# Query-key normed attention on one core: sums of squares on TensorE, four norm steps on GpSimd, a 22-column v, and another plan

## Chip, cores and metric

The kernel runs on one core of a Trainium2 chip. The metric is the device time of one execution in microseconds (us); where several runs were made, their median.

## What is computed

The reference normalizes q and k by their lengths over the last axis, multiplies the logits by a temperature per head, and does plain attention. There are 32 heads, 2048 rows and 20 columns per head; all inputs are bf16.

```python
qn = q / (jnp.sqrt((q * q).sum(axis=-1, keepdims=True)) + eps)
kn = k / (jnp.sqrt((k * k).sum(axis=-1, keepdims=True)) + eps)
logits = jnp.einsum('bhqd,bhkd->bhqk', qn, kn) * t[None, :, None, None]
attn = _softmax(logits, axis=-1)
return jnp.einsum('bhqk,bhkd->bhqd', attn, v)
```

## The kernel before

**Tiles.** Four heads form a group, so there are 8 groups; a group has 4 blocks of 512 queries. One unit of work is one head, one block of 512 queries and one strip of 128 keys: 8 x 4 x 4 x 16 = 2048 units. For each unit TensorE multiplies 128 keys by 512 queries (L692) into a bank of 512 fp32 columns. The columns of a head are padded from 20 to 32, so that four heads lie side by side on the 128 rows of `qT` and `kT`.

**Two ways to the exponential.** A unit takes one of two ways. In the first ("A"), two units form a wave in `psA`, and ScalarE turns the wave's 1024 columns into `pA` in one call (L885). In the second ("D"), the unit goes to one of three banks of `psD`; VectorE forms an int16 whose bits, read as fp16, are a rough exponential (`P1`, L325, result in `dI`), and two copies of it with a constant added (`S1` and `S2`, results in `dS`) mend the shape. These additions, called shifts below, are done by VectorE (L340, several units in one call) or by GpSimd (L338, as int32, so 256 columns for a unit's 512). The product with v (L714, "PV") is one matmul for an A unit and four for a D unit: `dI` with v, `dI` with half of v (`vhalf`), and the two `dS` with v. All of them add up in `psO`, 32 rows per head: 20 columns of v, one column of ones for the denominator, and zeros. At the end of a block VectorE transposes `psO` out (`drain`, L360), takes a reciprocal (`rec`, L364), and GpSimd multiplies (`omul`, L366).

**The preparation of a group** (`prep_ops`) is done while the group before it is computed: squares (`sq`, L260) and their sums over 20 columns (`red`, L263) on VectorE, eight small steps on 128 sums (`rs0` to `rs5`, `eps`, `inv`, L282 to L289) on VectorE, the scaling of k and q (L304) on GpSimd, and two DMA transposes issued from SP (L414). For the first group a shorter path through ScalarE's square root gets the first 512 rows going.

**A plan fixes the order.** `make_plan` runs through the kernel once in Python, with a clock of its own and a price for each operation, and from this it writes out one fixed order of instructions for each engine, with semaphore waits where data demand it. `step_pe0` picks the next matmuls, `step_dve` and `step_pool` the next work of VectorE and GpSimd, `step_sp` the next DMA. Two rules matter here. VectorE calls that read SBUF at more than one column per cycle keep GpSimd off SBUF (`o.port`); so the plan starts a GpSimd operation only beside a VectorE call that reads PSUM (`P1`, `drain`) and adds a wait for the call before that one. And small filler matmuls (`heat`, L558) are put in where TensorE would have too little to do, to keep its clock up. Which units go the D way is not written down anywhere: it comes out of the plan.

**Constants.** `NPA` is the number of `pA` slots, `RUN_MAX` the most units in one VectorE shift, `POOL_MAX` the most in one GpSimd shift, `PSLACK` how far a GpSimd operation may stand out beyond the VectorE call beside it, `PREP0`, `PREPN`, `PREP1` when the preparation is spread in, `LOAD1` when the loads of the second group start.

Of the kernel before, what the change touches and what calls it, by code (L numbers as in the profile page):

```python
# [6 lines left out]
BF16 = mybir.dt.bfloat16  # L7
# [34 lines left out]
PREP1 = (.25,.35)  # L42
# [3 lines left out]
HOLD = 0  # L46
# [7 lines left out]
POOL_MAX = 3  # L54
ALONE = (.2, 0)
PMIN = 5
PGAP = 0.3
PVHOLD = (.22,.22)
HEAT0 = 11
HEATN = 128  # L60
HEAT = .57
# [4 lines left out]
ACT0 = .05  # L66
ACT1 = .24
# [10 lines left out]
PSLACK = 0.15  # L78
# [3 lines left out]
SOON = 8  # L82
DURG = 1
LOAD1 = 0.2
DJOIN = 0.3
# [60 lines left out]
def bass_standalone__qk_norm__prompt_kernel(  # L146
# [15 lines left out]
    with ExitStack() as es:  # L162
# [16 lines left out]
        vaug = [sbuf(f"vaug{i}", [128, NH, R, 32], BF16) for i in range(2)]  # L179
        vpart = {c: [sbuf(f"v{n}{i}", [128, NH, R, 32], BF16) for i in range(2)] for c, n in ((.5, "half"),)}  # L180
# [7 lines left out]
        idn = sbuf("idn", [128, 128], BF16)  # L188
        nr0 = sbuf("nr0", [128, 2, NH, 4], F32)
# [41 lines left out]
        def prep_ops(hg, r0, r1, a0=0, a1=2, pool=False):  # L231
# [9 lines left out]
            for c0 in range(r0, r1, sqn * 2 // na):  # L241
# [30 lines left out]
            def add(nm, emit, reads, writes, rate=R1, fix=0.0):  # L272
                ops.append(dve(nm, n, rate, emit, reads, writes, fix))
# [5 lines left out]
            else:  # L279

                y = ri.bitcast(F32)
                add("rs0", lambda e: e.tensor_scalar(ri, s_.bitcast(I32), -0.5, RS_MAGIC, ALU.mult, ALU.add), [SS], [K("ri")], R2)  # L282
                add("rs1", lambda e: e.tensor_tensor(rb, s_, y, ALU.mult), [K("ri"), SS], [K("rb")])
# [58 lines left out]
        def part_op(hg, c):  # L342
            b = hg % 2
            f = lambda tl: tl[b][:, :, :, :].rearrange("p h r d -> p (h r d)")
            return dve("vh", NH * R * 32, R4, lambda e: e.tensor_single_scalar(f(vpart[c]), f(vaug), c, ALU.mult),
                       [("v", b, hh) for hh in range(NH)] + [("vz", b)], [("vh", b, c)])
# [33 lines left out]
        def load_qk(hg, a, part=None):  # L380
            b = hg % 2
            r0, r1 = (0, R) if part is None else PARTS[part]
            if a == 0 and hg == HG - 1:

                ops = []
                for x in range(4):
# [10 lines left out]
                        0.5, 4.0 if part != 0 else 2.2)]  # L397
# [10 lines left out]
        def tr_op(hg, which, r0, r1):  # L408
# [6 lines left out]
                       [(which + "pad", b, r) for r in range(r0, r1)], keys, 0.58 + 0.17 * (r1 - r0), 1.75 + 0.17 * (r1 - r0))  # L415
# [21 lines left out]
        def make_plan(share):  # L437
# [61 lines left out]
            def zeros(i, after=()):  # L499
                z = lambda ap_, val, key: Op("POOL", "z", lambda e: e.memset(ap_, val), after, [(key, i)], 0.5, 0.6)  # L500
                return [z(kpad[i][:, :, :, D:32], 0.0, "kz"), z(qpad[i][:, :, :, D:32], 0.0, "qz"),
                        z(vaug[i][:, :, :, D:D + 1], 1.0, "vz"), z(vaug[i][:, :, :, D + 1:32], 0.0, "vz")]
# [3 lines left out]
                               [], ["iot"], 0.5, 0.6)] + zeros(0))  # L506
# [54 lines left out]
            o = Op("PE", "heat", None, ["zt"], [("psA", 0)])  # L561
            o.info = [(lambda e, i=i: e.matmul(psA[:, (i % 3) * QW:(i % 3 + 1) * QW], zt[:, 0:128], zt[:, :])) for i in range(HEAT0)]
# [56 lines left out]
            if share:  # L619
                for c in vpart:  # L620
                    o = part_op(0, c)
                    o.reads.append(("qpad", 0, R - 1))
                    want_dve(o, 3)
            loaded = 1
            next_prep = []
            first_prep = [x[2] for x in dve_todo if x[2].name not in ("cp", "vh", "z")]
# [4 lines left out]
            def plan_group(hg):  # L631
# [9 lines left out]
                w_ = [o.cost if o.eng == "DVE" else PREPW * o.cost for o in po]  # L641
# [4 lines left out]
            def feed_prep():  # L646
                while next_prep:
# [10 lines left out]
                    want_dve(o, PRIO)  # L658
                    next_prep.pop(0)

# [6 lines left out]
            def pe_put(op, mode, strips):  # L667
# [5 lines left out]
                for hh in strips:  # L673
                    s0 = max(st, grp[hh])
                    grp[hh] = s0 + TS
# [5 lines left out]
                used_w.append((st, end, 0.25 * TS * len(strips) / (end - st)))  # L681
# [27 lines left out]
            def pv_mm(unit, rhs, first, last, coef):  # L709
# [3 lines left out]
                dst = psO[32 * hh:32 * hh + 32, :]  # L713
# [122 lines left out]
            def step_pe0():  # L836
# [73 lines left out]
                if pe_mode != "qk" and flying < DURG and not 0 < wait < DJOIN and step_qkd([], False):  # L910
                    return True
                if parts and not slot_free and before is not None and before.done is not None \
# [16 lines left out]

            def psd_free_at():  # L930
                rds = P.readers.get(("psD", issued_d % DBANKS), [])
# [4 lines left out]
            def step_qkd(used, with_a):  # L936
# [13 lines left out]
                def empty(i):  # L950
                    rds = P.readers.get(("psD", i), [])
                    return all(r.done is not None and r.done + SEML <= now for r in rds) and (rds or P.last_w.get(("psD", i)) is None)
# [379 lines left out]
```

## Time and profile before

| what | value |
|---|---|
| time, median of 3 runs | 632.86 us (632.52 to 632.88) |
| the profiled execution | 633.45 us |
| its span, first to last instruction | 631.5 us |
| granted TensorE clock, mean | 0.995 of full speed |
| units by ScalarE / by VectorE | 1333 / 715 |
| shifts (units x 2): VectorE / GpSimd | 703 / 727 |
| filler matmuls of 128 columns | 310 |

The page lists each engine's busy time, then groups of equal instructions by source line with their count, busy time, mean duration, and the idle time of the engine just before them with what ended it. "Busy" is the union of the intervals of a group, so it is smaller than count times mean where one call begins before the last has drained. The views by form keep tiles of different sizes apart. The profile's source lines are those of the kernel before; in the changed kernel ScalarE's exponential is L959, `P1` L356, the shifts L371 and L369, QK L766, PV L788 and the filler L591.

### The profile page before, as it was taken

What the parts mean: (1) busy time and instruction counts of PE and PEld (TensorE: products, weight loads), DVE (VectorE), ACT (ScalarE), POOL (GpSimd) and SP (SyncE); (2) the same over time, 40 slices, a digit from 0 to 9 for tenths busy, and PEclk for the clock granted to TensorE, in tenths of its full rate; (3) what the DMA queues carried; (4) which work ended last, traced back from release to release, by engine and by line L of the source; (5) the groups of instructions that cost most, each with busy time, mean ns of one, the idle gap of its engine ahead of it and who ended that gap; (6) DMA issues with size and microseconds to landing.
All of it is one profiled execution on the core that took longest, in us unless ns stands there. A gap on an engine that the chain in (4) does not pass through costs nothing.

```text
span 631.5 us, 15864 instructions
## 1 busy us (share of the span) xinstructions
PE 614.5 (97%) x6794; PEld 180.3 (29%) x6794; DVE 614.1 (97%) x869; ACT 618.8 (98%) x675; POOL 445.5 (71%) x491
## 2 busy tenths in 40 slices
PE   8999999999999999999999999999999999999996
PEld 4432222322222232223223222232222332222221
DVE  6999999999999999999999999999999999999995
ACT  6999999999999999999999999999999999999995
POOL 4586667766677776876768666776777777666772
PEclk8999999999999999999999999999999999999999
DMA  6610404041040130306031050400404022010000
GB/s 73 88 10 16 95 1 43 2 62 48 2 43 2 35 76 5 39 2 111 1 29 16 1 110 3 40 4 3 93 3 57 2 33 37 1 23 6 6 5 13
DMA packets 113772, 19.57 MB, mean 31 GB/s; under 512 B 102944, under 2 KB 113696, under 8 KB 113696
## 3 DMA queue, kind: packets, MB, share of 16 engines
q1 hardware_dynamic: 112896, 18.37, 19.9%
q8 instruction: 55, 0.90, 0.6%
q10 hardware_dynamic: 800, 0.12, 0.1%
q14 instruction: 21, 0.17, 0.1%
HBM read 7.87 MB, written 2.62 MB: 17 GB/s over the span
## 4 chain that ended last, share of the span: by engine, by line
ACT 72%; PE 26%; DVE 1%; DMA 0%; issue 0%; POOL 0%
ACT pA L885 72%; PE psO L714 12%; PE psA L692 10%; PE psD L692 2%; PE psO L558 2%; DMA qk<-in_q_dram 0%; DVE ssum L263 0%; POOL kpad L304 0%; DVE accT L360 0%; PE psD L570 0%; DVE sqs L260 0%; DVE ost L368 0%; DVE qT L585 0%; DVE rn L289 0%; DVE rec L364 0%
## 5 line engine op out<-in xcount | busy, mean ns | idle before, releaser
L885 ACT ACTIVATE pA<-psA 128x1024 f16<-128x1024 f32 (+1 forms) x667 | 614.5, 1111 | 2.0 <-PE psA L692 1.6
L338 POOL TENSOR_TENSOR dS<-dI,shc 128x256 int32<-128x256 int32 (+2 forms) x378 | 373.0, 1007 | 130.0 <-DVE dS L340 93.2
L325 DVE TENSOR_SCALAR dI<-psD 128x1024 int16<-128x1024 f32 (+1 forms) x486 | 434.1, 927 | 4.4 <-PE psD L692 1.8
L692 PE MATMUL psA<-qT,kT 32*128 32x512 bf16 x1553 | 283.0, 384 | 8.9 <-ACT pA L885 6.0
L714 PE MATMUL psO<-pA,vaug 128*32 128x512 f16 (+1 forms) x1333 | 233.7, 384 | 0.0
L714 PE MATMUL psO<-dS,vaug 128*32 128x512 f16 x1430 | 224.5, 385 | 0.0
L692 PE MATMUL psD<-qT,kT 32*128 32x512 bf16 x715 | 193.9, 383 | 0.0
L714 PE MATMUL psO<-dI,vaug 128*32 128x512 f16 x715 | 155.3, 386 | 0.0
L714 PE MATMUL psO<-dI,vhalf 128*32 128x512 f16 x715 | 152.0, 384 | 0.0
L692 PEld LDWEIGHTS psA<-qT,kT 32*128 32x128 bf16 x1553 | 69.0, 91 | 239.4 <-ACT pA L885 224.1
L340 DVE TENSOR_SCALAR dS<-dI 128x2048 int16<-128x2048 int16 (+2 forms) x182 | 122.5, 679 | 0.0
L714 PEld LDWEIGHTS psO<-dS,vaug 128*32 128x32 bf16 x1430 | 51.1, 94 | 73.2 <-issue 58.7
L714 PEld LDWEIGHTS psO<-pA,vaug 128*32 128x32 bf16 x1333 | 52.5, 94 | 37.5 <-issue 31.8
L692 PEld LDWEIGHTS psD<-qT,kT 32*128 32x128 bf16 x715 | 45.4, 91 | 22.1 <-DVE dI L325 10.2
L714 PEld LDWEIGHTS psO<-dI,vaug 128*32 128x32 bf16 x715 | 36.7, 93 | 24.5 <-issue 17.4
L714 PEld LDWEIGHTS psO<-dI,vhalf 128*32 128x32 bf16 x715 | 36.4, 94 | 22.0 <-issue 19.2
L366 POOL TENSOR_TENSOR ost<-accT,rec 128x320 bf16<-128x320 f32 x31 | 23.3, 753 | 16.7 <-DVE dS L340 9.5
L304 POOL TENSOR_TENSOR qpad<-qk,rn 128x320 bf16<-128x320 bf16 x31 | 22.0, 728 | 17.3 <-DVE dS L340 10.4
L558 PE MATMUL psO<-zt 128*128 128x128 bf16 x310 | 32.3, 228 | 0.1
L304 POOL TENSOR_TENSOR kpad<-qk,rn 128x320 bf16<-128x320 bf16 x31 | 22.2, 738 | 10.8 <-DVE dS L340 6.1
L558 PEld LDWEIGHTS psO<-zt 128*128 128x128 bf16 x310 | 19.7, 101 | 21.0 <-issue 20.1
L360 DVE STREAM_TRANSPOSE accT<-psO 128x512 f32<-128x512 f32 x32 | 22.6, 705 | 2.7 <-PE psO L714 2.7
(51 smaller groups left out, 100.1 us busy)
## 6 DMA issues: line engine op xcount, KB each, us to landing
vaug<-in_v_dram SPq DMA_DIRECT2D x32, 80.0 KB, 4.0
qk<-in_k_dram SPq DMA_DIRECT2D x7, 320.0 KB, 4.0
out_dram<-ost SPq DMA_DIRECT2D x28, 80.0 KB, 1.9
qk<-in_q_dram SPq DMA_DIRECT2D x6, 320.0 KB, 3.9
qk<-in_q_dram SPq DMA_DIRECT2D x4, 80.0 KB, 3.1
out_dram<-ost SPq DMA_DIRECT2D x7, 40.0 KB, 2.0
qk<-in_k_dram SPq DMA_DIRECT2D x1, 240.0 KB, 3.6
qk<-in_q_dram SPq DMA_DIRECT2D x1, 240.0 KB, 4.2
```

The costliest lines, as they stand in the source:

```text
L304: emit = lambda e, o=dst, x=src, s=sc: e.tensor_tensor(o, x, s, ALU.mult)
L325: lambda e: e.tensor_scalar(dst, psD[:, pb * QW:(pb + n) * QW], 1024.0 * LOG2E, 15360.0 - 1024.0 * LOG2K + SHIFTS[0], ALU.mult, ALU.add),
L338: lambda e: e.tensor_tensor(o.bitcast(I32), x.bitcast(I32), c, ALU.add), rd + ["shc"], wr)
L340: lambda e: e.tensor_single_scalar(o, x, float(SHIFTS[i] - SHIFTS[0]), ALU.add), rd, wr)
L360: dve("drain", QW, R1, lambda e: e.transpose(aT[:, :, :].rearrange("p b d -> p (b d)"), psO[:, :]), ["psO"], [("accT", b)], 0.03),
L366: pool_op("omul", 320, True, lambda e: e.tensor_tensor(dst, num, rcb, ALU.mult), [("accT", b), ("rec", b)], [("ost", ob, qg)]) if pool else
L558: return lambda e: e.matmul(bank, zt[:, 0:128], zt[:, 0:n], start=False, stop=False, skip_group_check=True)
L692: return lambda e: e.matmul(dst, lhsT, rhs, tile_position=(32 * hh, 0))
L714: return lambda e: e.matmul(dst, lhsT, rhs, start=first, stop=last, skip_group_check=True, tile_position=(0, 32 * hh))
L885: a = Op("ACT", "exp", lambda e, s=src, d=dst: e.activation(d, s, ACT.Exp), [("psA", slot)], [("pA", pslot, i) for i in range(WAVES[slot]) ...
```

## The change

- **Sums of squares on TensorE** for groups 1 to 7. VectorE still squares (two calls of 1280 columns per group), the squares go through two DMA transposes (`Ts`, SP queue) into `sqT`, and 20 matmuls of 32 columns against a 0/1 matrix `ind` add them up into a bank of `psD`, which is lent for that and given back when `rs0` and `rs1` have read it. The two `red` calls per group are gone. `ind` is made once at the start from an iota on GpSimd and two small VectorE calls.
- **Four norm steps on GpSimd** (`rs2`, `rs3`, `rs4`, `eps`) for these seven groups.
- **v in 22 columns** instead of 32: 20, the ones, and one zero. The rows 22 to 31 of each head in `psO` are never written by PV; a filler matmul at the very start writes zeros there.
- **The plan** gets GpSimd's late start (`PLAG`, and the end of the VectorE call before), an earlier release of VectorE (`LOCKL`), other prices for DMA (`LOAD0`, `TRL`, `TRK`), and other constants.
- **What comes out of the plan** (instructions on the path that runs):

| engine | instruction | before | after |
|---|---|---|---|
| ScalarE | exponential, 1024 / 512 columns | 666 / 1 | 662 / 0 |
| VectorE | `P1`, 1024 / 512 columns | 229 / 257 | 183 / 358 |
| VectorE | shifts: calls / units | 182 / 703 | 208 / 797 |
| GpSimd | shifts: calls / units | 378 / 727 | 454 / 651 |
| GpSimd | norm steps of 128 columns | 0 | 28 |
| TensorE | PV | 4193 | 4220 |
| TensorE | QK into psA / psD | 1553 / 715 | 1560 / 724 |
| TensorE | filler, 128 columns | 310 + 11 long | 188 + 12 long |
| TensorE | sums, 32 columns | 0 | 140 |
| SP | DMA transposes | 16 | 30 |

At the start, VectorE's order becomes squares, maximum over t (`flag`), sums, two calls for `ind`, `eps`; it was squares, sums, `flag`, `eps`. On SP the four loads of v for the second group now stand ahead of the first DMA transpose of `kT`, and the loads of its k and q ahead of those. On GpSimd a load of the operation library stands ahead of the first `rs3`; the kernel before has one such load, ahead of its iota.

```diff
-NPA = 20
+NPA = 18
+VW = 22
-RUN_MAX = 4
+RUN_MAX = 6
-D_END = 6
-D_LAST = 18
-D_WAIT = 36
+D_END = 4
+D_LAST = 14
+D_WAIT = 30
-PREP1 = (.25,.35)
+PREP1 = (.15,.45)
-POOL_MAX = 3
-ALONE = (.2, 0)
+POOL_MAX = 2
+ALONE = (.2,.2)
+LOAD0 = 2.75
+TRL = 2.25
+TRK = 1.2
+PLAG = .03
+LOCKL = 0.12
-PSLACK = 0.15
+PSLACK = 0.3
-LOAD1 = 0.2
+LOAD1 = 0
+NORM_POOL = ('rs2', 'rs3', 'rs4', 'eps')
...
-            for c0 in range(r0, r1, sqn * 2 // na):
+            bank = {}
+            for a in (1, 0) if hg else ():
+
+                sq, x3 = sqs[a][:, :], qk[b][:, a, :, :, :].rearrange("p h r d -> p (h r d)")
+                w_ = NH * R * D
+                keys = [("sqs", a)] + [("sqs", a, c) for c in range(R)]
+                ops.append(dve("sq", w_, R2, lambda e, o=sq, x=x3: e.tensor_tensor(o, x, x, ALU.mult),
+                               [("qk", b, a, i) for i in parts] + [("qkx", b, i) for i in range(1, 4)] * (a == 0), keys))
+                n_ = w_ // 128
+                dst = sqT[:, a * w_:(a + 1) * w_].rearrange("p (r n) -> p r n", n=128)
+                ops.append(dma("Ts", lambda e, o=dst, x=sq: e.dma_start_transpose(o, x), keys[:1], [("sqT", a)],
+                               0.58 + 0.17 * n_, TRL + 0.17 * n_))
...
             def add(nm, emit, reads, writes, rate=R1, fix=0.0):
-                ops.append(dve(nm, n, rate, emit, reads, writes, fix))
+                ops.append(pool_op(nm, n, rate != R2, emit, reads, writes) if pool and nm in NORM_POOL else
+                           dve(nm, n, rate, emit, reads, writes, fix))
...
+            def step_sums():
+                o = sums_todo[0]
+                for a in range(2):
+                    t_ = P.last_w[("sqT", a)]
+                    if t_.done is None or t_.done + SEML > now:
+                        return False
+                if "at" not in o:
+                    pb = next_bank()
+                    if not empty(pb):
+                        return False
+                    o["at"] = pb
+                    lent[0] += 1
+                    on_loan[:] = [o]
+                g, js = o["left"].pop(0)
+                dst = psD[:, o["at"] * QW + 32 * g:o["at"] * QW + 32 * g + 32]
+                mms = [lambda e, j=j: e.matmul(dst, sqT[:, (5 * g + j) * 128:(5 * g + j + 1) * 128], ind[:, 32 * j:32 * j + 32],
+                                               start=j == 0, stop=j == 4, skip_group_check=True) for j in js]
...
-                dst = psO[32 * hh:32 * hh + 32, :]
+                dst = psO[32 * hh:32 * hh + VW, :]
...
-                fits = lambda c: not busy or now + c <= end + PSLACK
+                st = max(now, on[-2].done + SEML + PLAG) if busy and len(on) > 1 else now
+                fits = lambda c: not busy or st + c <= end + PSLACK
...
-                finish(o, now, o.cost, o.lat)
-                free_["POOL"] = lock[0] = now + o.cost
+                finish(o, st, o.cost, o.lat)
+                free_["POOL"], lock[0] = st + o.cost, st + o.cost - LOCKL
```

More of the change, by code (lines that the diff above doesn't have):

```diff
@@ L45 @@
 DFIRST = 1
-HOLD = 0
+HOLD = 0.2
 DT = 0.005
@@ L640, in plan_group @@
                     po += [part_op(hg, c) for c in vpart]
-                w_ = [o.cost if o.eng == "DVE" else PREPW * o.cost for o in po]
+                w_ = [0 if isinstance(o, dict) else o.cost if o.eng == "DVE" else PREPW * o.cost if o.eng == "POOL" else 0 for o in po]
                 for j, o in enumerate(po):
@@ L949, in step_qkd @@
                     return False
[L950 to L953 removed]
+                pb = next_bank()
                 if not empty(pb):
```

96 lines of the change are left out of this document (72 added, 24 removed).

## The prediction

> **What bounds the kernel now.** I read the page's busy times first, then the groups of calls, then the waits.
>
> ```profile
> span 631.5 us, 15864 instructions
> PE 614.5 (97%) x6794; PEld 180.3 (29%) x6794; DVE 614.1 (97%) x869; ACT 618.8 (98%) x675; POOL 445.5 (71%) x491
> L885 ACT ACTIVATE pA<-psA 128x1024 f16<-128x1024 f32 (+1 forms) x667 | 614.5, 1111 | 2.0 <-PE psA L692 1.6
> ```
> ```profile
> L885 ACT ACTIVATE pA<-psA 128x512 f16<-128x512 f32 x1 | 0.7, 739 | 0.0
> ```
> ```profile
> 20.00:600.00 580.00, 571.89 (x6348) 164.77 (x6351) 576.08 (x788) 579.38 (x629) 421.00 (x453) 1.00 0.20 31
> ```
> ```profile
> PEld psA L692 <- ACT pA L885: 224.1, 552, 0.8
> ```
>
> Three engines show 97% or more, so shares don't name the bound. ScalarE's exponentials do: 667 calls, 614.5 us busy, and only 2.0 us of idle time before all of them. They run back to back, one per 614.5 / 666.5 = 0.922 us (counting the half-wide one as half). A kernel with the same calls can't end much sooner; one with fewer calls can. TensorE isn't the bound although it shows 97%: its weight loads waited 224.1 us for ScalarE to free `psA`, 0.34 us per wave. VectorE is nearly one: between 20 and 600 us (in the window's row its busy time is the third, ScalarE's the fourth) it idled 580 - 576.08 = 3.9 us, ScalarE 0.6 us. So the two are balanced to under 1%, and the plan's split of units is what balances them.
>
> **Term 1, the exponentials: -4.2 us.** The new plan sends 724 units to VectorE, so ScalarE makes 662 wide calls instead of 666 wide and one half-wide. A wide one is worth 0.922 us; the half-wide saves its shorter duration, 1.111 - 0.739 = 0.37, so it is worth 0.55. 4 x 0.922 + 0.55 = 4.24 us. It counts in full only as long as ScalarE stays fed.
>
> **Term 2, the start: +0.5 us.** The chain to the first exponential goes over VectorE.
>
> ```profile
> 1.28 0.48 SPq L529 DMA_DIRECT2D tb<-in_t_dram  x1
> 3.44 0.49 DVE L260 TENSOR_TENSOR sqs<-qk 128x640 bf16<-128x640 bf16 x1 [1.06 <-DMA qk<-in_q_dram]
> 3.97 0.82 DVE L263 TENSOR_REDUCE ssum<-sqs 128x32 f32<-128x640 bf16 x1
> 4.70 0.18 DVE L530 TENSOR_REDUCE tmx<-tb 128x1 f32<-128x32 bf16 x1
> 5.08 0.18 DVE L278 TENSOR_SCALAR rsa<-nr 128x32 f32<-128x32 f32 x1 [0.20 <-ACT nr L277]
> 8.39 1.94 ACT L885 ACTIVATE pA<-psA 128x1024 bf16<-128x1024 f32 x2 [0.32 <-PE psA L692]
> ```
> ```profile
> tb<-in_t_dram SPq DMA_DIRECT2D x1, 8.0 KB, 2.9
> ```
>
> Before, the sums began at 3.97, right behind the squares. Now `flag` stands between, and it waits for the load of t: issued at 1.28, landed 2.9 later, at 4.18. With its own 0.18 the sums begin near 4.40, 0.43 late. Behind them the two calls for `ind` (160 columns, about 0.3 and 0.25 us, an estimate from the 128-column rows of L286 and L285 below) end near 5.65, while `eps` would be ready at 4.40 + (5.08 - 3.97) = 5.51. So `eps` starts at about 5.6 instead of 5.08, and everything behind it moves: the scaling, the transposes, the first exponential. I take +0.5; bounds 0 (t lands before the squares end) and +0.75 (no call overlaps the next).
>
> **Term 3, VectorE's ledger: +0.4 us.** Its changed calls, by these rows:
>
> ```profile
> L325 DVE TENSOR_SCALAR dI<-psD 128x1024 int16<-128x1024 f32 x229 | 277.2, 1211 | 2.6 <-PE psD L692 1.3 <-PE psA L692 0.5
> L325 DVE TENSOR_SCALAR dI<-psD 128x512 int16<-128x512 f32 x257 | 171.7, 674 | 1.8 <-PE psO L558 0.8 <-PE psD L692 0.5
> L340 DVE TENSOR_SCALAR dS<-dI 128x2048 int16<-128x2048 int16 x165 | 114.3, 697 | 0.0
> L340 DVE TENSOR_SCALAR dS<-dI 128x1024 int16<-128x1024 int16 x8 | 3.4, 428 | 0.0
> L263 DVE TENSOR_REDUCE ssum<-sqs 128x64 f32<-128x1280 bf16 x14 | 20.6, 1474 | 0.0
> L286 DVE TENSOR_TENSOR ssum<-ssum,rsa 128x128 f32<-128x128 f32 x7 | 2.0, 291 | 0.0
> L284 DVE TENSOR_TENSOR rsa<-rsb,rsi 128x128 f32<-128x128 f32 x7 | 2.0, 285 | 0.0
> L285 DVE TENSOR_SCALAR ssum<-rsa 128x128 f32<-128x128 f32 x7 | 1.6, 227 | 0.0
> L288 DVE TENSOR_SCALAR rsa<-rsb 128x128 f32<-128x128 f32 x7 | 1.5, 221 | 0.0
> ```
> ```profile
> 149.36 0.68 DVE L340 TENSOR_SCALAR dS<-dI 128x2048 int16<-128x2048 int16 x1
> 149.96 1.81 DVE L325 TENSOR_SCALAR dI<-psD 128x1024 int16<-128x1024 f32 x2
> 151.69 0.68 DVE L340 TENSOR_SCALAR dS<-dI 128x2048 int16<-128x2048 int16 x1
> ```
>
> The timeline shows that a call starts 0.07 to 0.08 us before the last one has ended: a 2048 shift lasts 0.68 and holds the engine 0.60; a 1024 and a 512 `P1` together hold it 1.73, about 1.13 and 0.60. So I count each mean less 0.07:
> - `P1`: 101 more of 512 columns x 0.60, 46 fewer of 1024 x 1.13: +8.6.
> - Shifts: a unit costs (0.697 - 0.428) / 2 = 0.134 us. 94 more units x 0.134 and 26 more calls x 0.07: +14.4.
> - `red`: 14 x 1.40 gone: -19.6.
> - Four norm steps gone: 7 x (0.291 + 0.285 + 0.227 + 0.221 - 0.28) = -5.2.
> - `vhalf` on 640 fewer columns: 8 x 640 / 512 x 0.134 = -1.3.
> - `rs0` now from PSUM, no row for it: taken as 0.1 more than now, +0.7 (bounds 0 and 7 x 0.2); `ind` +0.5.
>
> The sum is -1.9 us, while ScalarE's work shrinks by 4.2. To keep up, VectorE must give up 4.2 - 1.9 = 2.3 us of the 3.9 us that it idled. If it gives all, the term is 0; if none, +2.3. I take +0.4, near the lower end: the idle time was waits for TensorE's `psD`, and TensorE has slack per wave.
>
> **What else moves.** *TensorE* gains 140 small matmuls, 27 PV and some switches and loses 122 fillers.
>
> ```profile
> L570 PE MATMUL psD<-idn,kpad 128*128 128x128 bf16 x4 | 0.4, 222 | 1.1 <-POOL kpad L304 1.1
> 19.55 0.45 PE L558 MATMUL psO<-zt 128*128 128x128 bf16 x5
> ```
>
> Four transposes behind one another took (0.4 - 0.222) / 3 = 0.06 us each, five fillers (0.45 - 0.23) / 4 = 0.055. So 140 x 0.06 - 122 x 0.055 + 27 / 4 x 0.38 (four heads at once, each as long as the QK in the row below, an upper bound) = +4 us, and some 28 changes of mode. The 224.1 us in which the weight loads waited cover it; uncovered, 4 us over 662 waves is 0.006 each. The 22-column weights change nothing that streams: PV still moves 512 columns.
>
> *DMA.* Fourteen transposes join SP's queue; TensorE's sums wait for them, and behind the sums stand QK and PV.
>
> ```profile
> 2.83 6.07 SPq L405 DMA_DIRECT2D vaug<-in_v_dram  x4
> 23.69 0.90 SPq L395 DMA_DIRECT2D qk<-in_k_dram  x1
> 25.20 6.68 SPq L405 DMA_DIRECT2D vaug<-in_v_dram  x4
> 21.38 0.38 PE L692 MATMUL psD<-qT,kT 32*128 32x512 bf16 x1
> ```
> ```profile
> DMA to landing us min/median/max: 3.7/4.3/6.0
> ```
>
> A transpose landed in 3.7 to 6.0 us (8 to 16 blocks); the plan reckons 2.25 + 10 x 0.17 = 3.95 for one of 10. A late one may stop TensorE by up to 2 us, of which the two waves in `psA` cover 1.84: 7 x 0 to 0.2, I take +0.1. The first `kT` transpose is now queued behind the second group's loads: v of the first ends at 8.90, k and q take 1.51 (23.69 to 25.20), four v 6.1 to 6.7, so it is issued near 16.8 and lands at 21.1 to 22.8. TensorE first needs it at 21.38 + 0.5 (the QK in the row, with the start's delay). Bounds 0 and +0.9; covered by the waves in `psA`, I take 0.
>
> *GpSimd* isn't the bound, but the shifts come from it.
>
> ```profile
> L338 POOL TENSOR_TENSOR dS<-dI,shc 128x768 int32<-128x768 int32 x113 | 165.2, 1466 | 70.8 <-DVE dS L340 45.6 <-DVE sqs L260 9.7 <-DVE rsb L283 2.5
> L338 POOL TENSOR_TENSOR dS<-dI,shc 128x512 int32<-128x512 int32 x123 | 127.7, 1039 | 47.9 <-DVE dS L340 39.5 <-DVE vhalf L345 2.4 <-DVE sqs L260 1.8
> L338 POOL TENSOR_TENSOR dS<-dI,shc 128x256 int32<-128x256 int32 x142 | 85.7, 612 | 11.3 <-DVE dS L340 8.1 <-DVE ssum L286 1.2 <-DVE ssum L285 1.0
> L315 POOL TENSOR_TENSOR rn<-rn,tb 128x64 f32<-128x64 f32 x7 | 2.3, 330 | 0.0
> ```
>
> Shifts: 257 x 0.612 + 197 x 1.039 = 362 us against 379 (165.2 + 127.7 + 85.7). The 28 norm steps of 128 columns lie between 0.330 (64 columns) and 0.612 (256): at 0.42 they cost 12. Net -5 us; their latency lies in a preparation that has most of a group's 75 us. I take 0.
>
> One more instruction stands in its queue: a load of the operation library, ahead of the first `rs3`.
>
> ```profile
> 0.83 0.24 POOL L504 IOTA iot<- 128x128 f32 x1 [0.39 <-POOLq L1317]
> ```
>
> The load that the kernel has now, ahead of the iota, left 0.39 us of idle time, and the iota took 0.24. I take 0 (bounds 0 and 0.39; GpSimd idles 130 us beside its shifts).
>
> **The sum**, against the profiled execution: 633.45 - 4.24 + 0.5 + 0.4 + 0.1 = 630.2 us. The median of the runs stood 0.6 below it, so I forecast **629.6 us**.
>
> **Rivals.**
> *A, VectorE is the bound.* It gives up none of its idle time: -1.9 + 0.5 = -1.4, so 632.0 profiled, **631.4** as median. For it: 99.3% busy between 20 and 600 us. Against: its idle time is made of waits, and ScalarE's 0.922 paces those too.
> *B, GpSimd is held by the library load.* The second load comes in mid run, and TensorE stops at a PV whose `dS` is late. By the nearest row (0.39 us) nothing is seen: **629.6**. In a sentence by itself: the Trainium skill, "GPSIMD Engine Reference", section "2.1 Instruction dispatch", says that the first call after a freshly loaded library pays about 6 us with no visible instruction; by that, an estimate, 5.95 - 1.84 of cover = +4.1 and 633.7 us. The trace so far speaks against it, since the iota followed its load within 0.39 us, though the library may have been there already.
> *C, slower: VectorE's shifts wait for GpSimd.* More and smaller GpSimd operations may stand out beyond the `P1` beside them, and the shift that follows on VectorE, which shares SBUF's port with GpSimd, is held. There are 208 such shifts.
>
> ```profile
> 299.53 1.81 DVE L325 TENSOR_SCALAR dI<-psD 128x1024 int16<-128x1024 f32 x2
> 299.69 1.47 POOL L338 TENSOR_TENSOR dS<-dI,shc 128x768 int32<-128x768 int32 x1 [0.72 <-DVE dS L340]
> ```
>
> An undisturbed 2048 shift takes 0.68, the mean is 0.697: 0.017 us is lost per shift now. At 0.03 more per shift it is 208 x 0.03 = 6.2, so -1.4 + 6.2 = +4.8: **637.7**. It makes the kernel slower from (1.4 + 1.3) / 208 = 0.013 us per shift on. Against it: GpSimd starts 0.16 us after the `P1` (row above); the old plan ignored that and let it stand out 0.15, the new one reckons 0.156 and allows 0.30, so the real overhang is the same.
>
> **From this to the numbers.** Within 0.2% (1.27 us) a measurement of this kernel can't tell a change. Forecast 0.50, A 0.20, B as the page has it 0.07, C 0.18, and 0.05 for better than the forecast (ScalarE's idle time at the start gone too, 628). Faster than 631.6: the forecast, the better case and most of A, 0.69; slower than 634.1: C and a little of B, 0.20; between them 0.11. The range 627.8 to 634.0 takes in the bounds of the terms, A, and B; the forecast's own is 628.6 to 630.8.
>
> **What would show it.** Right: 662 exponentials with 2 to 3.5 us of idle time before them, 0.92 us each; the first starting near 8.9 instead of 8.39; `P1` rows with no more idle time than now; no idle stretch on GpSimd at `rs3`. Wrong: over 5 us of idle time before the exponentials; 2048 shifts with a mean well over 0.70; weight loads for `ind` waiting on a DMA for microseconds; a PV waiting on `dS` near 45 us.

## The result and the profile after

| | before | after |
|---|---|---|
| median of 20 runs each, us | 632.79 | 637.07 |
| spread, us | 631.97 to 633.89 | 631.64 and up; one run took 2704.77 |
| ratio after / before, 95% interval | | 1.0057 [1.0040, 1.0074] |
| profiled execution, us (span) | 633.45 (631.5) | 644.17 (642.3) |

The changed kernel is slower by 0.6%, where 629.6 us was forecast. No trace shows what the run of 2704.77 us did; the median is not moved by it. The ratio is taken over the 16 faster executions of after, whose granted TensorE clock was 0.978 to 0.992; the profiled one, with 0.967, is among the slower, 7.1 us above the median, and so shows more of what follows than most runs have.

The granted clock in 40 slices, in tenths of full speed, on the page of before:

```profile
PEclk8999999999999999999999999999999999999999
```

The page of after: the span, the busy times, the granted clock, and the groups of the exponentials and of VectorE's `P1` (busy time, mean ns, then the idle time before them and who ended it).

```profile
span 642.3 us, 16161 instructions
PE 621.7 (97%) x6856; PEld 171.7 (27%) x6856; DVE 614.5 (96%) x910; ACT 617.6 (96%) x670; POOL 442.7 (69%) x596
PEclk9979999999996999999999799999999979999998
L959 ACT ACTIVATE pA<-psA 128x1024 f16<-128x1024 f32 (+1 forms) x662 | 613.3, 1100 | 13.0 <-PE psD L766 8.4
L356 DVE TENSOR_SCALAR dI<-psD 128x512 int16<-128x512 f32 (+1 forms) x541 | 440.6, 853 | 15.2 <-PE psD L766 13.1
```

The exponentials are 662, as planned, but they stood idle for 13.0 us, against 2.0 before, and both they and `P1` waited for TensorE. The clock row says why: four dips inside the span, where before has none behind its first slice. The windows of after show one of them (start and end, length, busy time of PE, PEld, DVE, ACT and POOL with counts, then the granted clock, the DMA share and GB/s):

```profile
186.00:188.00 2.00, 1.80 (x21) 0.72 (x19) 2.00 (x4) 2.00 (x3) 1.65 (x2) 1.00 0.00 0
188.00:190.00 2.00, 1.77 (x28) 0.92 (x26) 2.00 (x4) 2.00 (x3) 1.04 (x1) 1.00 0.00 0
190.00:192.00 2.00, 1.77 (x21) 0.54 (x18) 2.00 (x6) 2.00 (x3) 1.04 (x1) 0.72 0.03 8
192.00:194.00 2.00, 2.00 (x12) 0.41 (x9) 1.40 (x3) 1.73 (x3) 1.45 (x2) 0.50 0.02 4
```

TensorE's timeline in after at the same place (start, duration, operation, count; in brackets a wait and who ended it):

```profile
188.00 0.39 PE L788 MATMUL psO<-pA,vaug 128*22 128x512 f16 x2
188.32 0.29 PE L725 MATMUL psD<-ind,sqT 128*128 128x32 bf16 x5
188.55 0.39 PE L766 MATMUL psA<-qT,kT 32*128 32x512 bf16 x2
188.87 0.29 PE L725 MATMUL psD<-ind,sqT 128*128 128x32 bf16 x5
189.01 0.22 PE L591 MATMUL psO<-zt 128*128 128x128 bf16 x1
189.45 0.39 PE L766 MATMUL psA<-qT,kT 32*128 32x512 bf16 x2 [0.23 <-ACT pA L959]
189.53 0.39 PE L766 MATMUL psD<-qT,kT 32*128 32x512 bf16 x2
189.85 0.29 PE L725 MATMUL psD<-ind,sqT 128*128 128x32 bf16 x5
190.36 0.39 PE L766 MATMUL psA<-qT,kT 32*128 32x512 bf16 x2 [0.23 <-ACT pA L959]
190.69 0.29 PE L725 MATMUL psD<-ind,sqT 128*128 128x32 bf16 x5
190.91 0.60 PE L788 MATMUL psO<-dS,vaug 128*22 128x512 f16 x1
```

This is where the four groups of sums of squares run, one group per wave of exponentials. From the first group to the last a wave holds a pair of QK into `psA`, five matmuls of 32 columns, and in all one filler and one pair of QK into `psD`; there is no PV between 188.4 and 190.9. No wait longer than 0.23 us stands in these lines. Right behind the fourth group a matmul of 512 columns takes 0.60 us instead of 0.39: the clock has fallen to half. It stays there until about 204.5. TensorE is then busy all the time, and ScalarE waits for it, as its timeline in after shows at the first of the four places:

```profile
43.54 1.02 ACT L959 ACTIVATE pA<-psA 128x1024 f16<-128x1024 f32 x1 [0.51 <-PE psA L766]
45.05 1.02 ACT L959 ACTIVATE pA<-psA 128x1024 f16<-128x1024 f32 x1 [0.48 <-PE psD L766]
```

A wave that took 0.92 us takes 1.5. The four falls (40 to 48, 190 to 206, 350 to 362 and 522 to 530 us) each begin at one of the seven stretches of sums and hold 11.6 of the 13.0 us that ScalarE idled. Between them nothing is wrong (windows of after, same columns):

```profile
50.00:186.00 136.00, 133.81 (x1541) 36.12 (x1537) 135.74 (x194) 135.81 (x148) 96.54 (x128) 1.00 0.30 46
530.00:632.00 102.00, 100.56 (x1175) 26.79 (x1169) 101.56 (x141) 102.00 (x112) 76.52 (x102) 1.00 0.09 18
```

ScalarE works 135.81 of 136.00 and 102.00 of 102.00 us.

One more wait of after lies outside of the falls, near 22 us. Rows of its timeline, on SyncE's queue, TensorE and ScalarE:

```profile
18.05 2.16 SPq L445 DMA_TRANSPOSE kT<-kpad  x1
22.20 0.37 PE L766 MATMUL psD<-qT,kT 32*128 32x512 bf16 x1 [1.15 <-DVE dI L356]
22.65 3.77 ACT L959 ACTIVATE pA<-psA 128x1024 f16<-128x1024 f32 x4 [0.55 <-PE psD L766]
```

The first `kT` transpose is issued at 18.05. TensorE's QK on the second group's keys starts only at 22.20, after 1.15 us of idling; the bracket names `P1`, but the wait was for the transpose: it landed 4.0 us after its issue, at 22.05, while the bank was free near 20.9 (the same QK starts at 20.98 in h1_start, further on, where the transpose is issued at 13.92). ScalarE lost 0.55 us.

### The profile page after: what moved, and what is told of

Read it like the earlier page. It is cut to its first block, busy times and chain, and to the rows that moved or that the text cites. A ratio compares the mean times of both kernels' runs of the same rounds, so it can differ in the third digit from the quotient of the medians.

```text
span 642.3 us, 16161 instructions
## 1 busy us (share of the span) xinstructions
PE 621.7 (97%) x6856; PEld 171.7 (27%) x6856; DVE 614.5 (96%) x910; ACT 617.6 (96%) x670; POOL 442.7 (69%) x596
## 3 DMA queue, kind: packets, MB, share of 16 engines
HBM read 7.87 MB, written 2.62 MB: 16 GB/s over the span
## 4 chain that ended last, share of the span: by engine, by line
ACT 64%; PE 27%; DVE 6%; SPq 1%; DMA 1%; issue 0%
ACT pA L959 64%; PE psO L788 13%; PE psA L766 12%; DVE dI L356 4%; DVE dS L371 1%; PE psD L766 1%; PE psO L591 1%; SPq L436 1%; DMA vaug<-in_v_dram 1%; DVE accT L391 0%; SPq L426 0%; PE psD L725 0%; DVE vhalf L376 0%; DVE ost L399 0%; SPq L562 0%
## 5 line engine op out<-in xcount | busy, mean ns | idle before, releaser
L356 DVE TENSOR_SCALAR dI<-psD 128x512 int16<-128x512 f32 (+1 forms) x541 | 440.6, 853 | 15.2 <-PE psD L766 13.1
L369 POOL TENSOR_TENSOR dS<-dI,shc 128x512 int32<-128x512 int32 (+1 forms) x454 | 358.2, 797 | 136.0 <-DVE dS L371 93.2
L766 PE MATMUL psA<-qT,kT 32*128 32x512 bf16 x1560 | 288.5, 392 | 10.2 <-ACT pA L959 7.1
L788 PE MATMUL psO<-pA,vaug 128*22 128x512 f16 (+1 forms) x1324 | 249.9, 389 | 0.5 <-DMA vaug<-in_v_dram 0.5
L788 PE MATMUL psO<-dS,vaug 128*22 128x512 f16 x1448 | 240.0, 390 | 0.1
L788 PE MATMUL psO<-dI,vaug 128*22 128x512 f16 x724 | 167.9, 392 | 0.3
L788 PE MATMUL psO<-dI,vhalf 128*22 128x512 f16 x724 | 167.6, 391 | 0.0
L371 DVE TENSOR_SCALAR dS<-dI 128x3072 int16<-128x3072 int16 (+5 forms) x208 | 140.2, 687 | 0.1
L766 PEld LDWEIGHTS psA<-qT,kT 32*128 32x128 bf16 x1560 | 69.9, 92 | 259.2 <-ACT pA L959 232.4
L788 PEld LDWEIGHTS psO<-dS,vaug 128*22 128x22 bf16 x1448 | 50.6, 89 | 77.1 <-issue 64.9
L788 PEld LDWEIGHTS psO<-pA,vaug 128*22 128x22 bf16 x1324 | 50.9, 89 | 36.0 <-issue 29.7
L788 PEld LDWEIGHTS psO<-dI,vaug 128*22 128x22 bf16 x724 | 36.7, 89 | 27.0 <-issue 15.2
L788 PEld LDWEIGHTS psO<-dI,vhalf 128*22 128x22 bf16 x724 | 37.3, 90 | 22.8 <-issue 20.2
L335 POOL TENSOR_TENSOR qpad<-qk,rn 128x320 bf16<-128x320 bf16 x31 | 22.1, 727 | 16.8 <-DVE dS L371 10.9
```

Source lines behind the costliest of these rows:

```text
L335: emit = lambda e, o=dst, x=src, s=sc: e.tensor_tensor(o, x, s, ALU.mult)
L356: lambda e: e.tensor_scalar(dst, psD[:, pb * QW:(pb + n) * QW], 1024.0 * LOG2E, 15360.0 - 1024.0 * LOG2K + SHIFTS[0], ALU.mult, ALU.add),
L369: lambda e: e.tensor_tensor(o.bitcast(I32), x.bitcast(I32), c, ALU.add), rd + ["shc"], wr)
L371: lambda e: e.tensor_single_scalar(o, x, float(SHIFTS[i] - SHIFTS[0]), ALU.add), rd, wr)
L766: return lambda e: e.matmul(dst, lhsT, rhs, tile_position=(32 * hh, 0))
L788: return lambda e: e.matmul(dst, lhsT, rhs, start=first, stop=last, skip_group_check=True, tile_position=(0, 32 * hh))
```

## The experiments

Theory S: the stretches of sums are too thin to hold TensorE's clock, and all that the change lost is there. Its rivals: the 22-column weights of PV let the clock go (C); something else of the change, VectorE or GpSimd, costs the time, and the falls come by chance. Each ratio is against the kernel before, run in the same session.

**The changed kernel again (e0_after).** No edit.

> The changed kernel as it is. In the profiled execution TensorE's granted clock fell to half four times, for 5 to 15 us each, and each fall began while the four groups of sums matmuls ran. Theory S (the sums stretch leaves TensorE with too little work, and the clock gate halves its clock): falls again, in some of the seven sums stretches and nowhere else, mean clock below 0.992, time 633 to 640 us and different from run to run. Theory C (PV with 22 instead of 32 weight columns counts as less activity): falls too, but not bound to the sums. Rival C of the prediction (VectorE's shifts are held by GpSimd): a mean of the 2048 shifts and of P1 above those of before also where the clock is full.

Measured: 637.4 us median, ratio 1.0071 [1.0041, 1.0102]. In the profiled execution the clock fell at 42 to 48 and 346 to 362 us, both at sums, and once more near the start, at 9 to 13 us, where the profile of before has a fall too (8 to 11 us). So behind the start the falls return at the same kind of place, but not at each place each time. The "nowhere else" of the expectation does not hold for the start.

**Fillers beside the sums (e1_fill).** Same plan and order as after. Behind each of the 28 groups of sums stand two matmuls on zeros, 256 columns each, into an unused part of the bank that the sums have on loan:

```diff
-                op.info = mms
+                rest = psD[:, o["at"] * QW + 256:o["at"] * QW + 512]
+                op.info = mms + 2 * [lambda e: e.matmul(rest, zt[:, 0:128], zt[:, 0:256], start=True, stop=True, skip_group_check=True)]
```

> Same plan and same order on every engine; behind each of the 28 groups of sums matmuls stand two filler matmuls of 256 columns, which write zeros into unused columns of the lent bank (0.21 us of TensorE time each pair). S: no falls of the clock (0.995 as before the change), 629.5 us (629.0 to 630.3), faster than the kernel before by 0.4 to 0.6%. C: the falls stay, or most of them, 633 us or more. Rival C of the prediction: as slow as the changed kernel.

Measured: 630.58 us, 0.3 above the expected range, ratio 0.9962 [0.9942, 0.9983]. More work on TensorE made the kernel 6.8 us faster than e0_after, and faster than before. The page of e1_fill:

```profile
span 628.6 us, 16273 instructions
PE 611.1 (97%) x6912; PEld 172.4 (27%) x6912; DVE 613.9 (98%) x910; ACT 615.8 (98%) x670; POOL 442.3 (70%) x596
PEclk9999999999999999999999999999999999999999
L960 ACT ACTIVATE pA<-psA 128x1024 f16<-128x1024 f32 (+1 forms) x662 | 611.5, 1099 | 1.9 <-PE psA L767 1.3
L356 DVE TENSOR_SCALAR dI<-psD 128x512 int16<-128x512 f32 (+1 forms) x541 | 439.6, 854 | 2.5 <-PE psD L767 0.9
```

No dip in the clock row, 1.9 us of idle time before the same 662 exponentials instead of 13.0, and `P1` waits 2.5 instead of 15.2. Theory S is shown: fillers at the sums and nowhere else, and the loss is gone. The clock isn't safe in every run: ten of the 12 had 0.995 or more, the other two 0.992 and 0.988 (632.82 and 635.47 us), as one of the 29 runs of before had 0.987 (638.34 us). Where these three fell, no trace shows.

**A quarter of the dose (f4_small_fill).** One filler of 128 columns per group:

```diff
-                op.info = mms + 2 * [lambda e: e.matmul(rest, zt[:, 0:128], zt[:, 0:256], ...)]
+                op.info = mms + 1 * [lambda e: e.matmul(rest, zt[:, 0:128], zt[:, 0:128], ...)]
```

> The plan of e1_fill and after, with one filler of 128 columns per group of sums (28 in all) instead of two of 256, a quarter of the columns. If what counts is TensorE's busy share over a stretch, a filler of 0.055 us in waves of 0.92 us moves it by 6 points against 23 in e1_fill (two of about 0.11): the clock still falls to 0.5 in some of the four places, median 634 to 637, ratio 1.002 to 1.006. If any streamed matmul of 128 rows and 128 columns in the wave keeps the clock: 630.6, ratio 0.996, no fall.

Measured: 630.75 us, ratio 0.9978 [0.9964, 0.9992], and no fall in the profiled execution before its end. The median is that of the second expectation. But 5 of its 12 runs had a granted clock under 0.994 (631.2 to 633.9 us), against 2 of 12 with the larger fillers and all 7 of e0_after. It is far from e0_after; 5 against 2 is too few to tell it from e1_fill. The thinnest 2 us in the same stretch, windows of f4_small_fill, of e1_fill and of after:

```profile
187.00:189.00 2.00, 1.74 (x29) 0.86 (x25) 2.00 (x5) 2.00 (x4) 1.10 (x2) 1.00 0.00 0
```
```profile
187.00:189.00 2.00, 2.00 (x30) 1.01 (x28) 2.00 (x5) 2.00 (x4) 1.10 (x2) 1.00 0.00 0
```
```profile
189.00:191.00 2.00, 1.55 (x26) 0.82 (x24) 2.00 (x5) 2.00 (x4) 1.10 (x2) 0.96 0.03 8
```

PE is busy 1.74, 2.00 and 1.55 of 2.00 us. This share doesn't decide a single stretch, though: in after the clock held behind the stretch at 124 us, whose last 2 us had 1.52, and in i3_heat70, further on, it fell where PE was busy 1.90. What amount of work is enough isn't shown.

**v in 32 columns again (e2_v32).** The planner still reckons with 22, so that the order stays the same.

```diff
-VW = 22
+VW = 32
...
-            return dve("vh", NH * R * VW, R4, ...
+            return dve("vh", NH * R * 22, R4, ...
```

> Same plan and order, but v and half v have 32 columns again (zeros in the last 11), so PV loads 32 weight columns. S: no help, 634 to 639 us with falls in the sums stretches. C: no falls, 629.5 to 630.5 us.

Measured: 638.66 us, ratio 1.0099 [1.0061, 1.0137], with falls at 40 to 48 and 190 to 206 us, both at sums. The 22 columns aren't the cause: C is out.

**Sums back on VectorE (e3_dve_sums).** The rest of the change is kept; planned anew it has 718 units and 665 exponentials.

```diff
-            for a in (1, 0) if hg else ():
+            for a in ():
...
-            if hg:
-                ops.append(bank)
-            for c0 in range(r0, r1, sqn * 2 // na) if not hg else ():
+            for c0 in range(r0, r1, sqn * 2 // na):
...
-                sums = lambda: psD[:, ...].rearrange("p (h r) -> p h r", r=R) if hg else s_
+                sums = lambda: psD[:, ...].rearrange("p (h r) -> p h r", r=R) if "at" in bank else s_
```

> The sums of squares go back to VectorE for all groups (no transposes of squares, no sums matmuls, no lent bank); all else of the change stays. The plan then has 718 units for VectorE and 665 exponentials. S: no falls of the clock, 629.5 + 3 x 0.92 = 632.3 us (631.5 to 633). C: falls stay, 635 us or more. Rival C of the prediction: slower than 634 with a full clock.

Measured: 637.2 us, ratio 1.0069 [1.0041, 1.0096]; the expectation is missed. The reading has two parts. Nine of its 14 runs lie at 636.3 to 637.4 us with a clock of 0.995 or more, so there something other than the clock costs some 4 us (next experiment). The other five took 644.6 to 652.76 us; the profiled execution is one of these, with no fall at the places of the sums, but with one long fall. TensorE's timeline and a window of e3_dve_sums:

```profile
22.24 0.37 PE L764 MATMUL psD<-qT,kT 32*128 32x512 bf16 x1 [1.38 <-DMA kT<-kpad]
...
22.90 0.24 PE L589 MATMUL psO<-zt 128*128 128x128 bf16 x1
23.07 0.60 PE L764 MATMUL psD<-qT,kT 32*128 32x512 bf16 x1
```
```profile
24.00:64.00 40.00, 40.00 (x254) 11.27 (x251) 25.80 (x32) 26.82 (x27) 19.38 (x25) 0.50 0.03 5
```

It began 0.8 us after the late `kT` transpose had stopped TensorE for 1.38 us, and it held for 40 us in which TensorE was busy 40.00: at half clock it can't catch up, and ScalarE worked 26.82 of 40.00. So the sums aren't the only place at which the change puts the clock at risk: after has the same late transpose, with a stop of 1.15 us and no fall in its profile.

**The same without that stop (f6_dve_sums_start).** Loads of the second group's v behind the first `kT` transpose, the flag and one call for `ind` later; 715 units and 667 exponentials, as before has.

```diff
-LOAD1 = 0
+LOAD1 = 0.2
...
-                want_dve(dve("flag", ..., ["tb"], ["flag"]), 1.4)
+                want_dve(dve("flag", ..., ["tb"], ["flag"]), 1.6)
...
-            want_dve(dve("ind", 160, R1, ..., ["iof"], ["iof"]), 4)
+            want_dve(dve("ind", 160, R1, ..., ["iof", ("kpad", 0, 4)], ["iof"]), 4)
```

> As e3_dve_sums (sums of squares on VectorE, all else of the change kept), but the first kT transpose is issued ahead of the second group's loads of v and the flag stands behind the sums, so that TensorE doesn't wait near 22 us; planned anew it has 715 units on VectorE and 667 exponentials, as before has. No fall near 22 us in any theory that names the late transpose. At full clock, ScalarE as the bound: 667 x 0.922 as in before: 633.0, ratio 1.000, ScalarE idle under 3 us. VectorE as the bound: by the rows of after its calls cost red +19.6, P1 -6.3, shifts -8.4, so +4.9 us against e1_fill, of which its 2.5 us of idle time take up half at most: 633.0 to 635.5, ratio 1.000 to 1.004, with ScalarE idle 3 to 5 us, waiting on TensorE's QK. By the same count e3_dve_sums has +7.5 us and 636 to 638, which its runs at full clock had.

Measured: 634.73 us (634.22 to 635.16), ratio 1.0033 [1.0021, 1.0044], within VectorE's range and outside of ScalarE's 633.0. All six runs had a clock of 0.997 or more. This kernel has no late transpose, no sums on TensorE and 363 fillers, and no run fell; which of the three keeps the clock it doesn't tell. It does show that the change without its sums on TensorE is slower than the kernel before even at full clock, with the same number of exponentials. What doesn't fit: ScalarE's idle time was 1.5 us, where 3 to 5 were expected. The profiled execution is 1.3 us longer than that of before (632.8 against 631.5 us of span): 0.23 of it at the start (first exponential at 8.62 instead of 8.39) and 0.95 behind the last exponential (7.87 us instead of 6.92), where VectorE ends its last units. Of VectorE as the bound this fits only the end; that VectorE is what costs the time here is argued, not shown.

**Norm steps back on VectorE (f3_fill_norm_dve).** The fillers of e1_fill stay; 723 units, 663 exponentials.

```diff
-NORM_POOL = ('rs2', 'rs3', 'rs4', 'eps')
+NORM_POOL = ()
```

> The fillers of e1_fill, with the four norm steps per group back on VectorE; planned anew it has 723 units on VectorE and 663 exponentials. If GpSimd's norm steps relieve VectorE and VectorE is near its bound: norm steps +5.2, P1 0, shifts -2.0, so +3.2 us on VectorE, against its 2.5 us of idle time, and one exponential more: 631.5 to 634.0, ratio 0.998 to 1.002. If ScalarE alone sets the time: 630.6 + 0.9 = 631.5, ratio 0.998. If the norm steps on GpSimd held up shifts there (the slower rival of the forecast), taking them away makes it faster: under 630, ratio under 0.995.

Measured: 634.89 us, ratio 1.0041 [1.0028, 1.0054], 0.9 us beyond the range for VectorE near its bound. The four of its six runs with a clock of 0.995 or more lie at 634.6 to 634.9 us, some 4 us above e1_fill. So the move of four steps to GpSimd, with the one exponential that it saves and the plan that comes with it, is worth some 4 us, and the theory that these steps hold up GpSimd is out. The profiled execution (638.93 us) had a fall from 22.8 to 33.1 us, right where the late `kT` transpose had stopped TensorE for 1.84 us, so its rows aren't read for the other runs. Stops there of 1.38 (e3_dve_sums) and 1.84 us went with a fall, stops of 1.05 (e1_fill) and 1.15 us (after) did not.

**A better start (h1_start).** e1_fill with the flag behind the first sums and the loads as in f6: 726 units, 661 exponentials.

```diff
-LOAD1 = 0
+LOAD1 = 0.2
...
-                want_dve(dve("flag", ..., ["tb"], ["flag"]), 1.4)
...
+            want_dve(dve("flag", ..., ["tb", ("ssum", 0, (0, 0, 2))], ["flag"]), 1.4)
```

> The version with the fillers of e1_fill, in which VectorE's flag no longer stands ahead of the first group's sums (it waits for them), and in which the loads of the second group's v queue behind the first kT transpose; planned anew it has 726 units on VectorE and 661 exponentials instead of 724 and 662. If the forecast's ledger holds once TensorE's clock is held: one exponential fewer (-0.92), a first exponential about 0.4 us earlier and the 0.55 us which the late kT transpose cost gone, from 630.6 us: 628.7, ratio 0.993, first exponential near 8.4 and no idle time of ScalarE near 22 us. If VectorE is already the bound at 724 units: its changed calls by the rows of after (P1 +1.5, shifts +0.1) come on top and the saved exponential is worth nothing: 630.6 - 0.9 + 1.6 = 631.3, ratio 0.997, with over 3 us of idle time of ScalarE.

Measured: 635.79 us, ratio 1.0087 [1.0049, 1.0124]; neither number came. The edits did what they were meant to do: the first exponential starts at 8.49 (8.60 in e1_fill), and the wait near 22 us is gone, as ScalarE's timeline in h1_start shows.

```profile
20.11 6.59 ACT L960 ACTIVATE pA<-psA 128x1024 f16<-128x1024 f32 x7
```

But the plan used the room for two more units on VectorE. The page of h1_start:

```profile
span 633.2 us, 16269 instructions
PE 614.4 (97%) x6901; PEld 173.8 (27%) x6901; DVE 618.2 (98%) x934; ACT 616.0 (97%) x669; POOL 445.4 (70%) x599
L960 ACT ACTIVATE pA<-psA 128x1024 f16<-128x1024 f32 (+1 forms) x661 | 611.7, 1093 | 3.7 <-PE psA L767 2.8
L371 DVE TENSOR_SCALAR dS<-dI 128x1536 int16<-128x1536 int16 (+5 forms) x225 | 145.3, 661 | 0.1
```

VectorE's busy time grew by 618.2 - 613.9 = 4.3 us, where 1.6 was counted, and ScalarE idles 3.7 us. VectorE also ends later than ScalarE: the span ends 9.5 us behind the last exponential, in e1_fill 6.7. Of the 4.6 us by which the span is longer, 1.8 are idle time and 2.8 the end. This fits a VectorE that is at its bound at 724 units already; that the new order has a part in it is not ruled out.

**The flag alone (h4_flag).** The plan of e1_fill; only the flag's edit of h1_start.

> The plan of e1_fill (724 units, 662 exponentials, the same fillers) with one edit: VectorE's flag stands behind the first group's sums and no longer ahead of them, so that the sums don't wait for the load of t. If the start counts in full once the clock holds: the sums near 4.0 instead of 4.41, the first exponential 0.1 to 0.4 us earlier than in e1_fill, where it began at 8.60: 630.2 to 630.5, ratio 0.996. If VectorE binds at 724 units: its calls are the same, only begun earlier, so it gains no less; a median over 631.5 would speak against both. The start alone can't bring more than 0.5 us.

Measured: 631.65 us, ratio 0.9981 [0.9962, 0.9999], above the 631.5 that was to speak against both expectations; the clock is why. Six of 12 runs lie at 629.86 to 630.48 us with a clock of 0.998 or more, as e1_fill's do at such a clock (629.71 to 630.49): the first exponential began only 0.10 us earlier (8.50), and a gain of that size can't be told from none. The other six had 0.993 or less and took 632.8 to 639.8 us. The profiled execution is one of these, and fell here (timeline and window of h4_flag):

```profile
11.95 0.40 PE L789 MATMUL psO<-pA,vaug 128*22 128x512 bf16 x4 [0.91 <-DMA vaug<-in_v_dram]
...
13.63 0.61 PE L789 MATMUL psO<-pA,vaug 128*22 128x512 f16 x4
```
```profile
12.00:26.00 14.00, 14.00 (x99) 6.06 (x99) 6.72 (x19) 9.62 (x11) 3.81 (x5) 0.56 0.63 80
```

TensorE had waited 0.91 us for the first v. The same wait of 0.91 us stands in e1_fill's trace without a fall, so whether the flag's place has a part in it, or it is chance, stays open.

**More fillers everywhere (i3_heat70).** The changed kernel; only the planner's limit for fillers is raised.

```diff
-HEAT = 0.58
+HEAT = 0.70
```

> The changed kernel without the fillers in the lent bank; instead the planner's own limit for fillers is raised from 0.58 to 0.70, which sets 324 fillers of 128 columns instead of 188, almost all outside of the stretches in which the sums run (722 units on VectorE, 663 exponentials). If it is the thin stretch itself that lets the clock go: falls at the sums as before, 636 to 638, ratio 1.005 to 1.009, clock under 0.99. If the clock goes because the whole run is too near a limit: no falls, 630.6 + 0.9 = 631.5, ratio 0.998.

Measured: 646.02 us, ratio 1.0199 [1.0184, 1.0213], beyond both. Most of it isn't the clock: ScalarE idles 13.8 us, of which one stop is 9.3 us. The new plan itself leaves TensorE 63 fillers there in place of work, since a group's `qT` comes late. So the time decides nothing. The trace of i3_heat70 does tell one thing, at a stretch of sums (TensorE's timeline, two windows, and ScalarE's timeline with the long stop):

```profile
121.64 0.31 PE L725 MATMUL psD<-ind,sqT 128*128 128x32 bf16 x5
121.88 0.61 PE L788 MATMUL psO<-dI,vaug 128*22 128x512 f16 x4
```
```profile
118.00:120.00 2.00, 1.90 (x20) 0.70 (x19) 2.00 (x4) 2.00 (x3) 1.57 (x3) 1.00 0.00 0
120.00:122.00 2.00, 1.92 (x28) 0.91 (x25) 2.00 (x6) 2.00 (x4) 1.32 (x2) 0.85 0.03 8
```
```profile
562.35 4.69 ACT L959 ACTIVATE pA<-psA 128x1024 f16<-128x1024 f32 x5 [9.31 <-PE psD L766]
```

Even with 324 fillers in the plan instead of 188 the clock fell at the end of a stretch of sums, at one of the seven in this execution, with PE busy 1.90 of the 2 us before. Fillers elsewhere don't fully replace those in the stretch.

## Why the prediction was wrong

The forecast was 629.6 us with 0.69 for faster. The arithmetic leads to 630.58, which e1_fill has; after lies 6.5 us above that. So 1.0 us of the miss lies in the terms that the forecast had, and 6.5 us in one that it left out, TensorE's clock.

**The step that failed** is the part on TensorE in "What else moves". It sized the 140 matmuls and the 122 fillers that go as time on an engine with slack: "The 224.1 us in which the weight loads waited cover it". In time that holds: in after the weight loads still waited 232.4 us for ScalarE (its waits: total, times, longest).

```profile
PEld psA L766 <- ACT pA L959: 232.4, 564, 0.8
```

But work on TensorE isn't there for its time alone. It keeps the clock, and the change sets four waves with little work in a row, seven times. What the sum put at nothing cost 6.5 us: e1_fill, with 28 pairs of fillers in these stretches, has it back. Of the planner's own fillers e1_fill has the same 188 as after, so the 122 that went aren't what was missed; the stretches are. None of the rivals named the clock; 637.7 us of rival C is near the result by chance, with another mechanism. And the sums' own matmuls hardly count as work: five of 32 columns last 0.29 us with 0.176 for one, so they start (0.29 - 0.176) / 4 = 0.028 us apart. The planner's own bookkeeping, which weighs them by 0.3, did not prevent the falls either.

The Trainium skill, "TensorE: Matmul & The Clock Gate", section "HAM oscillation — how this bites in real kernels", gives as the rule that the clock falls with idle gaps of more than about 3.4 us on TensorE. The falls here go beyond it: in the stretch at 188 us no wait was over 0.23 us, and the clock fell. Nearer to them is its section "A second HAM failure mode: psum-queue depth-cycling", a kernel in which short idle times between groups of matmuls were enough. The same page's section "What's actually happening" says that the window in which the activity is watched runs freely; that not every stretch of sums falls in every run (four of seven in the profiled execution, two in e0_after) fits it, and so does the grid on which the clock changes (last section).

**Term 1 (-4.2)** was the right mechanism, too large: e1_fill's exponentials were busy 611.5 us against 614.5, so -3.0. One took 611.5 / 662 = 0.9237 us instead of 0.9220. The 1.2 us that are missing are as much as the whole difference between 629.6 and e1_fill, 1.0 us.

**Term 2 (+0.5)** came as told: the flag waited for t, the first exponential is at 8.81 in after (0.42 late), at 8.60 in e1_fill.

**Term 3 (+0.4)**: VectorE's work was to change by -1.9 us; from before to e1_fill its busy time changed by 613.9 - 614.1 = -0.2. `P1` gave up 4.4 - 2.5 = 1.9 of its idle time. The term itself came out near 0, as ScalarE's idle time is 1.9 us against 2.0. But "nearly a bound" may have been an understatement: f3 and h1, with 3.2 us more for VectorE by count and 4.3 by measurement, are 4 to 5 us slower than e1_fill, of which one exponential explains 0.9 in f3 and none in h1. Each was planned anew, so this is not a proof.

**DMA**: the transposes of squares held TensorE up nowhere (0, not 0.1). The first `kT` transpose was issued at 18.05, not 16.8, and cost 0.55 us, within the bounds 0 and 0.9, where 0 was taken because "covered by the waves in `psA`"; it landed at 22.05, inside the forecast's 21.1 to 22.8 (whose lower end should be 20.5 by the row's minimum of 3.7) but behind the 21.9 at which TensorE needed it. It also stopped TensorE where its clock could fall (e3, f3).

**GpSimd** came as told: shifts 358.2 us (362 forecast), norm steps 0.30 to 0.53 us each (0.42). Rival B is out; GpSimd's timeline in e1_fill, where the clock holds, at the first norm steps:

```profile
44.55 1.04 POOL L369 TENSOR_TENSOR dS<-dI,shc 128x512 int32<-128x512 int32 x1
45.68 0.30 POOL L316 TENSOR_SCALAR ssum<-rsa 128x128 f32<-128x128 f32 x1
```

The first `rs3` (L316) starts 0.09 us behind the shift before it. Of the 6 us that the Trainium skill, "GPSIMD Engine Reference", section "2.1 Instruction dispatch", has for a first call, this trace shows nothing.

Of what was to show it wrong, "over 5 us of idle time before the exponentials" came true, and so did one more: the 2048 shifts had a mean "well over 0.70".

```profile
L371 DVE TENSOR_SCALAR dS<-dI 128x2048 int16<-128x2048 int16 x15 | 11.1, 742 | 0.0
```

There are only 15 of them in after, and e1_fill, which is fast, has the same 15 at 0.741. So the longer shifts are real, but rival C's sum, 0.03 us on each of 208, isn't what made after slow. The other two signs did not appear.

## What to carry to other kernels

A filler, or any work on an engine with slack, isn't priced by its time alone where the engine's clock depends on its work: before you replace work on TensorE, look at what is left in each stretch of a few us, and read the granted clock in windows of 2 us beside the busy time. Where small matmuls stand in a row, put wide ones between them: 28 pairs of fillers, into columns that nobody used, turned +0.6% into -0.4%. Where two engines are both near their bound, what the planner does with spare room has to be measured: h1_start, with one exponential fewer, took 635.0 to 635.9 us in its runs at full clock, e1_fill 629.7 to 631.6.

## What was unexpected of the hardware

- The clock fell to 0.50 with no wait over 0.23 us, in stretches where PE was still busy 1.5 to 1.8 of each 2.00 us by the profile; with 28 matmuls of 128 columns more it held in the traced run of f4_small_fill.
- The clock changes on a grid. A fall's length follows from the windows of 2 us as 2 x (1 - clock) / 0.5, summed: from 190 to 206 us in after 2 x (0.28 + 6 x 0.50 + 0.13) / 0.5 = 13.6 us. The four falls of after last 6.8, 13.6, 10.2 and 6.8 us, those of e0_after 3.4, 3.4 and 13.6, that of e3_dve_sums 40.96: 2, 4, 3, 2, 1, 1, 4 and 12 times 40.96 / 12 = 3.413 us. And the later falls of after begin 150.2, 160.4 and 170.7 us behind the one before, 44, 47 and 50 times as much. So a fall costs whole steps of 3.413 us, and how a stretch lies on the grid, which differs from run to run, may decide whether it falls; that last part is not tested.
- Once fallen, it stayed for 6.8 to 13.6 us in after and for 41 us in e3_dve_sums, though TensorE was busy 40.00 of 40.00 us there. By the Trainium skill, "TensorE: Matmul & The Clock Gate", section "What's actually happening", some 3.4 us of sustained work bring it back; by the profile's busy time this trace differs. What ended the fall isn't shown.
- The time of an exponential isn't fixed: 0.9220 us before, 615.0 / 666.5 = 0.9227 in f6_dve_sums_start, 0.9237 in e1_fill, 611.7 / 661 = 0.9254 in h1_start, longer where VectorE has more units (715, 715, 724, 726). That the two engines hinder each other is only argued.
